# The softmax epsilon as a 65th column of the exponentials, in a kernel of attention, gated MoE and a second MoE

## The chip, the cores and the metric

One NeuronCore of a Trainium2 chip runs the whole program. The metric is the device time of one launch in microseconds (us). The engines that the text names are TensorE (PE, matrix products and transposes), VectorE (DVE), ScalarE (ACT), GpSimd (POOL) and SyncE (SP, which here only issues DMAs). All data are fp32; the large products run as three products of split numbers (a high and a low part).

## The reference

The first stage is the one that the change touches. Each batch entry and head has 768 queries, cut into chunks of 32; a chunk attends to a context of 56 keys (16 to the left, its own 32, 8 to the right) and to 8 memory keys, so 64 columns per head and query.

```python
scores = scale * np.matmul(q_c, k_full.transpose(0, 1, 3, 2))
scores = scores - np.max(scores, axis=-1, keepdims=True)
a = np.exp(scores)
a = a / (np.sum(a, axis=-1, keepdims=True) + 1e-09)
out[:, :, c_start:c_end] = np.matmul(a, v_full)
...
gate = 1.0 / (1.0 + np.exp(-(x @ w_gate)))
val = x @ w_val
x = gate * val @ w_out
...
h = x @ w_in
g = h * (1.0 / (1.0 + np.exp(-1.702 * h)))
return (g @ w_out).astype(np.float32)
```

There are 4 batch entries and 8 heads of width 64. The two later stages work on 3072 rows of width 512, with inner widths of 1536 and 2048.

## The kernel before

**Attention.** The function `attention` works on one of 32 tiles: 96 query rows, all 8 heads. PE transposes q and k (L436, L444), ACT copies them out of PSUM into `qt` and `kt` (L451, L456, L457), and PE computes the scores into the pair of PSUM banks `both` (L555). Then DVE takes the row maximum (L572) and subtracts it into the SBUF tile `e`, [96, 2, 4, 64] floats (L575); ACT makes exponentials of `e` in place (L580); DVE sums them per row and head into `sm` (L612), adds 1e-9 (L614) and inverts `sm` (L615). POOL, and for one 32-row band DVE, multiply `e` by `sm` into the padded tile `pw` (L623); PE transposes that (L645), ACT copies it to `pt` (L652), and PE multiplies by v (L704). The result is split into a high part on ACT (`xh`, L758) and a low part on DVE (`xl`, L761).

**Stages.** The six tiles of the first row block are the prologue. They have buffers of their own (`pro_bufs`, L886 to L892, where `pw` is cleared), except that the first of them uses the `e` of the set `main` (L870). The first product of the gated MoE (`first_product`, L821 and L828) needs all of them. From there on PE runs dense: gate and value products, the gate on ACT and DVE (L845, L848, L853), the output product (`gemm2`, L1020), and later the second MoE, whose two products are done in Strassen's manner (L1318, L1655). The other 26 tiles run beside this dense work, and all use the one `e` of `main`. Results of the gated MoE go out through two stages `f2`, used in turn: ACT copies a PSUM bank into a stage (L1040) and issues its store to `y_dram` (L1044).

**What sets the order.** All instructions are handed to a planner, the class `Schedule`. Each gets an engine, an estimated duration and keys that it reads and writes; the planner works out due times from the end backwards, simulates the engines by those estimates, and writes out one fixed order per engine. So each engine's queue is static, and one changed estimate can move instructions everywhere. Into gaps that the planner expects on PE ahead of the first product it puts fill products (L885), whose results nobody reads; their number is fixed in the program. In the trace one fill shows as two records.

SBUF is handed out in the order in which tiles are asked for. `e` of `main` is followed by `mx`, `sm`, `pt`, a pad of 112 floats (L871), and then by the slots of the weights and of what takes their place later. So all of these stand behind `e` at fixed distances.

Of the kernel before, what the change touches and what calls it, by code (L numbers as in the profile page):

```python
# [14 lines left out]
AF = mybir.ActivationFunctionType  # L15
ALU = mybir.AluOpType
# [6 lines left out]
TQ = CH * NCK  # L23
# [10 lines left out]
class Schedule:  # L34
# [9 lines left out]
    def add(self, eng, dur, fn, r=(), w=(), nbytes=0, due=None, slack=0.0, margin=0.0, hold=0.0):  # L44
        i = len(self.tasks)
        deps = set()
        for x in r:
            if x in self.writer:
                deps.add(self.writer[x])
        for x in w:  # L50
            if x in self.writer:
                deps.add(self.writer[x])
            deps.update(self.readers.get(x, ()))
        for x in r:
            self.readers.setdefault(x, set()).add(i)
        for x in w:
            self.writer[x] = i
            self.readers[x] = set()
        deps.discard(i)
        self.tasks.append(  # L60
            dict(eng=eng, dur=dur, fn=fn, deps=deps, nbytes=nbytes, due=due, slack=slack, margin=margin, hold=hold, succ=[])
        )
        return i
# [82 lines left out]
def kernel(  # L146
# [14 lines left out]
    nc = tc.nc  # L161
# [8 lines left out]
    NP = H // 2  # L170
    TPB = S // TQ
    NTILE = B * TPB
    KW = CTX + NM
    assert TK + NM == P and KW == 2 * CH and D == 2 * CH
    SCALE = 1.0 / float(D) ** 0.5
# [176 lines left out]
    class Bufs:  # L352


        def __init__(self, pool, suf, names, base=None):
            shapes = {
                "qn": [TQ, H, D],
                "kn": [P, H, D],
                "vn": [P, H, D],
                "qt": [P, NP, TQ],  # L360
                "kt": [P, NP, NCK, KW],
                "e": [TQ, 2, NP, KW],
                "mx": [TQ, 2, NP, 1],
                "sm": [TQ, H, 1],
                "pw": [TQ, H, P],
                "pt": [P, H, TQ],
                "qb": [P, NP, NCK, CH],
                "kb": [P, NP, 2 * NCK + 1, CH],
                "mn": [P, NP, CH],
                "mt": [P, NP, CH],  # L370
                "pn": [TQ, H, 3 * CH],
            }
            self.t = dict(base.t) if base else {}
            self.k = dict(base.k) if base else {}
            for n in names:
                self.t[n] = pool.tile(shapes[n], F32, tag=n + suf, name=n + suf)
                self.k[n] = n + suf
# [12 lines left out]
    def attention(t, bufs, banks, pe_path, extra=None, nth=0, last=False):  # L390
# [8 lines left out]
        kk = bufs.k  # L399
        T = bufs.t  # L400

        def tadd(eng, dur, fn, r=(), w=(), more=0.0, **kw):
            add(eng, dur, fn, r=r, w=w, slack=SL + more, **kw)
# [63 lines left out]
        else:  # L467
# [35 lines left out]
            if fresh:  # L503
                for hp in range(2):
# [9 lines left out]
                    w=[kk["mt"]],  # L514
# [48 lines left out]
        def scores():  # L563
            return both[:TQ, :, : NP * KW].rearrange("s a (p k) -> s a p k", k=KW)
# [8 lines left out]

        def ev_sub():
            nc.vector.tensor_tensor(  # L575
                out=T["e"], in0=scores(), in1=T["mx"].to_broadcast([TQ, 2, NP, KW]), op=ALU.subtract
            )

        def ev_exp():
            nc.scalar.activation(T["e"], T["e"], AF.Exp, scale=SCALE)  # L580

        def e3():
            return T["e"].rearrange("s a p k -> s (a p) k")
# [5 lines left out]
        else:  # L589
# [16 lines left out]
        d_sm = 0.64 if pe_path else 0.68  # L606
        tadd("dve", d_sm + edge, ev_max, r=kb01, w=[(kk["mx"], 0)])
        tadd("dve", d_sm, ev_sub, r=kb01 + [(kk["mx"], 0)], w=[(kk["e"], 0), (kk["e"], 1)])
        ke = [(kk["e"], 0), (kk["e"], 1)]
        tadd("act", c_act(512), ev_exp, w=ke)  # L610
        tadd(
            "dve", 0.6, lambda: nc.vector.tensor_reduce(out=T["sm"], in_=e3(), axis=AX.X, op=ALU.add), r=ke, w=[kk["sm"]]  # L612
        )
        tadd("dve", 0.07, lambda: nc.vector.tensor_scalar_add(T["sm"], T["sm"], 1e-9), w=[kk["sm"]])  # L614
        tadd("dve", 0.12, lambda: nc.vector.reciprocal(T["sm"], T["sm"]), w=[kk["sm"]])  # L615

        L = TQ - CH
# [269 lines left out]
    for i in range(NPRO):  # L887
        names = ["qn", "kn", "pw"] + (["vn", "qt", "kt", "e", "mx", "sm", "pt"] if i else [])
        x = Bufs(pro, f"_{i}", names, None if i else main)
        x.gate, x.ident, x.kid = None, lambda: ident["pro"], "ident"  # L890
        pro_bufs.append(x)
        (nc.gpsimd if i < 2 else nc.vector).memset(x.t["pw"], 0.0)  # L892

    pa = Bufs(pro, "", [], main)
    pa.k.update(qn="qn_a", kn="kn_a", pw="pw_a")
# [2 lines left out]
    for i in range(4):  # L898
        x = Bufs(pro, "", [], main)
# [52 lines left out]
    def attend(ts, bufs, banks):  # L952
        for t in ts:
            attention(t, bufs(t), banks(t), True)
# [25 lines left out]
    for i in range(2):  # L980
        for blk in (0, 2 * NCK):
            x = pb[2 * i]
# [18 lines left out]
    def attention_b(b):  # L1001
        for t in waves[b]:
            n = walk.index(t)
            before = walk[n - 1] if n else None
            x = pb[(t // 2) % 2 * 2 + t % 2]
            head = before is None or t % 2 == 0
            fresh = before is None or before // TPB != t // TPB
            extra = (0 if head else NCK, 2 - t % 2 if head else 0, fresh)
            attention(t, x, (A0, A1), False, extra, n, n == len(walk) - 1)
# [536 lines left out]
    a0, e, bb, a1 = sets[0]  # L1546
# [285 lines left out]
    a0, e, bb, a1 = AB  # L1832
# [67 lines left out]
```

## Time and profile before

| what | us |
|---|---|
| three runs | 1128.82, 1130.36, 1129.59 |
| median | 1129.59 |
| the profiled execution, its own time | 1130.38 |
| its span, from the first to the last instruction | 1128.6 |
| PE busy (99% of the span) | 1116.4 |
| DVE busy (75%) | 842.4 |
| ACT busy (52%) | 589.6 |
| POOL busy (14%) | 161.6 |
| first product of the dense phase starts at | 36.55 |

The mean granted clock of PE is 0.999 of full speed (2.4 GHz). Start times below count from the start of the span. An instruction's length can overlap the next one's start by about 0.1 us, since engines are pipelined: what an instruction takes of its engine's time is best read from its start to the next start.

### The profile page before, as it was taken

What the parts mean: (1) busy time and instruction counts of PE and PEld (TensorE: products, weight loads), DVE (VectorE), ACT (ScalarE), POOL (GpSimd) and SP (SyncE); (2) the same over time, 40 slices, a digit from 0 to 9 for tenths busy, and PEclk for the clock granted to TensorE, in tenths of its full rate; (3) what the DMA queues carried; (4) which work ended last, traced back from release to release, by engine and by line L of the source; (5) the groups of instructions that cost most, each with busy time, mean ns of one, the idle gap of its engine ahead of it and who ended that gap; (6) DMA issues with size and microseconds to landing.
All of it is one profiled execution on the core that took longest, in us unless ns stands there. A gap on an engine that the chain in (4) does not pass through costs nothing.

```text
span 1128.6 us, 19515 instructions
## 1 busy us (share of the span) xinstructions
PE 1116.4 (99%) x7190; PEld 933.7 (83%) x7190; DVE 842.4 (75%) x1440; ACT 589.6 (52%) x972; POOL 161.6 (14%) x209
## 2 busy tenths in 40 slices
PE   7999999999999999999999999999999999999998
PEld 6888899997888888888888888888888888888886
DVE  7989746776767788888887788869966369575365
ACT  5888632222222344676666777666455365354452
POOL 4332244122333113200001110000000000000000
PEclk9999999999999999999999999999999999999999
DMA  9676344335433555542556867868796666776526
GB/s 208 203 216 196 90 122 114 52 67 119 102 83 79 150 145 174 199 161 104 177 178 245 305 216 269 271 244 295 245 255 211 200 203 219 233 216 204 170 86 176
DMA packets 245903, 203.13 MB, mean 180 GB/s; under 512 B 170928, under 2 KB 191920, under 8 KB 245808
## 3 DMA queue, kind: packets, MB, share of 16 engines
q1 hardware_dynamic: 201560, 162.29, 48.9%
q0 software_dynamic: 6880, 24.12, 5.7%
q10 hardware_dynamic: 37368, 15.47, 5.0%
q8 instruction: 57, 0.93, 0.3%
q14 instruction: 38, 0.31, 0.1%
HBM read 151.49 MB, written 50.33 MB: 179 GB/s over the span
## 4 chain that ended last, share of the span: by engine, by line
PE 97%; DMA 1%; SPq 1%; ACT 0%; DVE 0%; issue 0%; ACTq 0%
PE bank L1318 30%; PE bank L1655 20%; PE bank L1020 18%; PE bank L821 15%; PE bank L828 8%; PE both L704 2%; PE both L555 2%; SPq L350 1%; PE bank L704 1%; PE bank L885 0%; DMA kn<-in_mem_k_dram 0%; PE bank L645 0%; DMA vn<-in_v_dram 0%; DMA w<-wo_dram 0%; PE both L645 0%
## 5 line engine op out<-in xcount | busy, mean ns | idle before, releaser
L1318 PE MATMUL bank<-sb_x,sb_r 128*128 128x512 f32 x1512 | 347.4, 389 | 0.0
L1318 PEld LDWEIGHTS bank<-sb_x,sb_r 128*128 128x128 f32 x1512 | 283.8, 188 | 58.9
L1655 PE MATMUL bank<-wq,w 128*128 128x512 f32 x756 | 178.0, 389 | 0.4 <-DMA w<-wo_dram 0.4
L1655 PEld LDWEIGHTS bank<-wq,w 128*128 128x128 f32 x756 | 141.8, 188 | 30.3 <-issue 0.8
L821 PE MATMUL bank<-xh,w 128*128 128x512 f32 (+1 forms) x464 | 159.6, 355 | 0.0
L821 PE MATMUL bank<-xl,w 128*128 128x512 f32 (+1 forms) x464 | 158.6, 353 | 0.0
L1334 DVE TENSOR_TENSOR sb_s<-bank,sb_s 128x512 f32<-128x512 f32 x108 | 74.4, 690 | 83.0 <-PE bank L1318 75.8
L828 PE MATMUL bank<-xh,w 128*128 128x512 f32 (+1 forms) x464 | 108.8, 356 | 0.0
L1020 PE MATMUL bank<-gh,wq 128*128 128x512 f32 (+1 forms) x448 | 98.7, 360 | 0.0
L821 PEld LDWEIGHTS bank<-xh,w 128*128 128x128 f32 x464 | 87.8, 189 | 12.6
L821 PEld LDWEIGHTS bank<-xl,w 128*128 128x128 f32 x464 | 87.8, 189 | 11.9
L1330 ACT ACTIVATE sb_s<-bank 128x512 f32<-128x512 f32 x108 | 64.8, 604 | 50.7 <-PE bank L1318 49.9
L828 PEld LDWEIGHTS bank<-xh,w 128*128 128x128 f32 x464 | 78.1, 189 | 12.4
L1020 PEld LDWEIGHTS bank<-gh,wq 128*128 128x128 f32 x448 | 76.4, 189 | 12.9
L670 DVE STREAM_TRANSPOSE pt<-raw 32x256 f32<-32x256 f32 x184 | 79.5, 432 | 4.7 <-POOL raw L623 2.1
L1626 DVE TENSOR_TENSOR wq<-xh_g,wq 128x1024 fp32r<-128x1024 f32 (+1 forms) x60 | 60.5, 1008 | 22.9 <-ACT wq L1623 22.5
L1623 ACT ACTIVATE wq<-xh_g 128x1024 fp32r<-128x1024 f32 (+1 forms) x60 | 53.3, 889 | 35.2 <-PE bank L1655 34.2
L853 ACT ACTIVATE gh<-sig 128x512 fp32r<-128x512 f32 (+1 forms) x58 | 32.3, 557 | 67.4 <-DVE sig L848 61.6
L623 POOL TENSOR_TENSOR raw<-e,sm 96x448 f32<-96x448 f32 (+2 forms) x69 | 41.0, 606 | 176.1 <-DVE sm L615 149.0
L1655 PE MATMUL bank<-wq,w_e 128*128 128x512 f32 x252 | 62.5, 389 | 0.0
L845 ACT ACTIVATE sig<-bank 128x512 f32<-128x512 f32 (+1 forms) x58 | 30.5, 526 | 55.5 <-PE bank L828 49.7
L1655 PEld LDWEIGHTS bank<-wq,w_e 128*128 128x128 f32 x252 | 47.3, 188 | 9.8
(215 smaller groups left out, 1646.1 us busy)
## 6 DMA issues: line engine op xcount, KB each, us to landing
sb_r<-wc_dram SPq DMA_DIRECT2D x133, 256.0 KB
w<-wo_dram SPq DMA_DIRECT2D x63, 512.0 KB
w_e<-wo_dram SPq DMA_DIRECT2D x21, 512.0 KB
wc_dram<-sb_r SPq DMA_DIRECT2D x15, 512.0 KB
wo_dram<-w POOLq DMA_DIRECT2D x14, 512.0 KB, 3.9
raw<-in_moe_w_out_dram SPq DMA_DIRECT2D x13, 512.0 KB
raw<-in_moe_w_in_dram SPq DMA_DIRECT2D x13, 512.0 KB
wf_dram<-f POOLq DMA_DIRECT2D x24, 256.0 KB, 2.9
```

The costliest lines, as they stand in the source:

```text
L623: eng.tensor_tensor(out=dst, in0=e3()[r, :, c], in1=T["sm"][r].to_broadcast([n, H, keys[1] - keys[0]]), op=ALU.mult)
L670: nc.vector.transpose(T["pt"][r * CH : (r + 1) * CH, :, c * CH : (c + 1) * CH], T["pn"][c * CH : (c + 1) * CH, :, kb * CH : (kb + 1) * CH],)
L704: nc.tensor.matmul((bk if to is None else to)[hp * D : (hp + 1) * D, o : o + q], T["vn"][:, 2 * p + hp, :], T["pt"][:, hp * NP + p, :q], s ...
L821: nc.tensor.matmul(bank[bk][:, :n], w[:, 0, ts[t]], x[xb][:, t, c0 : c0 + n], start=t == 0 and x is xhs, stop=False)
L828: nc.tensor.matmul(bank[bk][:, :n], w[:, 1, ts[t]], xhs[xb][:, t, c0 : c0 + n], start=False, stop=t == NK - 1)
L1020: nc.tensor.matmul(bank[into[m]][:, c0 : c0 + n], w[:, wi, m * P : (m + 1) * P], g[:, :n], start=f == 0 and j == 0 and c0 == 0, stop=f == ...
L1318: nc.tensor.matmul(bank[bk], w[:, o : o + P], xt[x, k][:, xl, :], start=first and k == 0 and wl == 0 and xl == 0, stop=k == 1 and wl == 1, ...
L1330: add("act", c_act(BLK), lambda: nc.scalar.activation(work[n], bank[bk], AF.Copy), r=[("bank", bk)], w=[n])
L1334: nc.vector.tensor_tensor(out=work[n], in0=bank[bk], in1=work[n], op=ALU.add)
L1623: nc.scalar.activation(quad[b_][:, c, 0, :], src(js), AF.Copy)
L1626: nc.vector.tensor_tensor(out=quad[b_][:, c, 1, :], in0=src(js), in1=quad[b_][:, c, 0, :].bitcast(F32), op=ALU.subtract)
L1655: nc.tensor.matmul(bank[bk], lhs, quad[b_][:, x, gl_, :], start=begin, stop=last and x == js[-1] and wl == 1, skip_group_check=not first,)
```

## The change

The tile `e` becomes 65 columns wide per head. The subtraction and the exponential write columns 0 to 63 through the view `e4()`. Column 64 holds the constant 1e-9, set once per buffer by a small memset on DVE ahead of everything else (six buffers: the five of the prologue and `main`'s, which the 26 later tiles share). The sum reads 65 columns, and the addition (L614) and its estimate in the planner are gone.

```diff
-                "e": [TQ, 2, NP, KW],
+                "e": [TQ, 2, NP, KW + 1],
...
         def ev_sub():
             nc.vector.tensor_tensor(
-                out=T["e"], in0=scores(), in1=T["mx"].to_broadcast([TQ, 2, NP, KW]), op=ALU.subtract
+                out=e4(), in0=scores(), in1=T["mx"].to_broadcast([TQ, 2, NP, KW]), op=ALU.subtract
             )
 
         def ev_exp():
-            nc.scalar.activation(T["e"], T["e"], AF.Exp, scale=SCALE)
+            nc.scalar.activation(e4(), e4(), AF.Exp, scale=SCALE)
+
+        def e4():
+            return T["e"][:, :, :, 0:KW]
...
-        tadd("dve", 0.07, lambda: nc.vector.tensor_scalar_add(T["sm"], T["sm"], 1e-9), w=[kk["sm"]])
         tadd("dve", 0.12, lambda: nc.vector.reciprocal(T["sm"], T["sm"]), w=[kk["sm"]])
...
         (nc.gpsimd if i < 2 else nc.vector).memset(x.t["pw"], 0.0)
+        nc.vector.memset(x.t["e"][:, :, :, KW : KW + 1], 1e-9)
```

Two things follow from it that the diff does not show. `e` takes 2080 bytes of each partition rather than 2048, so every tile behind `main`'s `e` stands 32 bytes further on. And the planner writes another order. Line numbers behind the change are 2 or 3 higher (the sum is L612 before and L615 after, the inversion L615 and L617, the fills L885 and L887).

DVE, the first three tiles of the prologue, before (`e`, `e_129`, `e_140` are the exponentials of tiles 0, 1 and 2, and so with `mx` and `sm`):

```order
9 L572 TENSOR_REDUCE mx_130<-both 96x8
10 L614 TENSOR_SCALAR sm<-sm 96x8
11 L575 TENSOR_TENSOR e_129<-both,mx_130 96x512
12 L615 RECIPROCAL sm<-sm 96x8
13 L612 TENSOR_REDUCE sm_131<-e_129 96x8
14 L572 TENSOR_REDUCE mx_141<-both 96x8
15 L614 TENSOR_SCALAR sm_131<-sm_131 96x8
16 L575 TENSOR_TENSOR e_140<-both,mx_141 96x512
17 L615 RECIPROCAL sm_131<-sm_131 96x8
```

The same place after (`e_130` and `e_142` are now those of tiles 1 and 2):

```order
15 L572 TENSOR_REDUCE mx_131<-both 96x8
16 L617 RECIPROCAL sm<-sm 96x8
17 L575 TENSOR_TENSOR e_130<-both,mx_131 96x8x64
18 L615 TENSOR_REDUCE sm_132<-e_130 96x8
19 L572 TENSOR_REDUCE mx_143<-both 96x8
20 L617 RECIPROCAL sm_132<-sm_132 96x8
21 L575 TENSOR_TENSOR e_142<-both,mx_143 96x8x64
```

The inversion now stands where the addition stood, ahead of the next tile's subtraction rather than behind it. The six memsets are rows 1 to 10 of DVE's queue, between those of `pw`.

PE, tiles 3 and 4 of the prologue, before (`pw_121` and `pw_125` are the probabilities of tiles 0 and 1, `qn_156`/`kn_157` q and k of tile 4, the L555 of row 23 its scores):

```order
17 L555 MATMUL both<-kt_150,qt_149 32x64 x24
18 L436 MATMUL bank_70<-ident,qn_156 128x96 x4
19 L444 MATMUL bank_71<-ident,kn_157 128x128 x4
20 L645 MATMUL bank_72<-ident,pw_121 128x96 x4
21 L645 MATMUL bank_73<-ident,pw_121 128x96 x4
22 L885 MATMUL bank_69<-ident 128x128
23 L555 MATMUL both<-kt_161,qt_160 32x64 x24
24 L704 MATMUL bank_68<-pt,vn 64x96 x8
25 L645 MATMUL bank_72<-ident,pw_125 128x96 x4
26 L645 MATMUL bank_73<-ident,pw_125 128x96 x4
```

After:

```order
17 L555 MATMUL both<-kt_153,qt_152 32x64 x24
18 L647 MATMUL bank_72<-ident,pw_121 128x96 x4
19 L647 MATMUL bank_73<-ident,pw_121 128x96 x4
20 L444 MATMUL bank_71<-ident,kn_161 128x128 x4
21 L436 MATMUL bank_70<-ident,qn_160 128x96 x4
22 L706 MATMUL bank_68<-pt,vn 64x96 x8
23 L647 MATMUL bank_72<-ident,pw_126 128x96 x4
24 L647 MATMUL bank_73<-ident,pw_126 128x96 x4
25 L555 MATMUL both<-kt_165,qt_164 32x64 x24
```

The transposes of tile 0's probabilities move ahead of those of tile 4's q and k, its scores behind tile 1's probabilities, and a fill goes. Over the whole prologue PE's queue has 33 fills after and 35 before; all other products are the same in number.

ACT at about 675 us of the trace before, where one row block of the gated MoE leaves through the two stages `f2` (here `f_83`) beside the first products of the second MoE (L1330 copies their banks out, L1841 works on their results):

```order
698 L296 ACTIVATE f_81<-raw_79 128x512
699 L1841 ACTIVATE xh_g<-sb_s_5380 128x512
700 L1841 ACTIVATE xl_g<-sb_s_5381 128x512
701 L1330 ACTIVATE sb_s_5380<-bank_73 128x512
702 L1330 ACTIVATE sb_s_5382<-bank_71 128x512
703 L1044 DMA y_dram<-f_83 128x512
704 L1040 ACTIVATE f_83<-bank_5332 128x512
705 L1261 ACTIVATE sb_r_5372<-f_81 128x2x256
706 L1841 ACTIVATE xh_g<-sb_s_5380 128x512
707 L1330 ACTIVATE sb_s_5381<-bank_73 128x512
```

After (L1043 and L1047 are the copy into a stage and its store):

```order
697 L296 ACTIVATE f_81<-raw_79 128x512
698 L1047 DMA y_dram<-f_83 128x512
699 L1043 ACTIVATE f_83<-bank_5305 128x512
700 L1844 ACTIVATE xh_g<-sb_s_5338 128x512
701 L1844 ACTIVATE xl_g<-sb_s_5339 128x512
702 L1333 ACTIVATE sb_s_5338<-bank_73 128x512
703 L1333 ACTIVATE sb_s_5340<-bank_71 128x512
704 L1264 ACTIVATE sb_r_5344<-f_81 128x2x256
705 L1844 ACTIVATE xh_g<-sb_s_5338 128x512
706 L1043 ACTIVATE f_83<-bank_5304 128x512
707 L1333 ACTIVATE sb_s_5338<-bank_70 128x512
708 L1333 ACTIVATE sb_s_5339<-bank_73 128x512
```

The first store is issued four instructions earlier, and the third copy into a stage (row 706), which stood at row 714 before, now stands ahead of two copies that free banks for PE.

## Rows read from the trace of the kernel before

**Rows 1.** The page: busy time by engine, and the chain that ended last

```profile
PE 1116.4 (99%) x7190; PEld 933.7 (83%) x7190; DVE 842.4 (75%) x1440; ACT 589.6 (52%) x972; POOL 161.6 (14%) x209
...
PE 97%; DMA 1%; SPq 1%; ACT 0%; DVE 0%; issue 0%; ACTq 0%
```

**Rows 2.** Waits of PE, all of the span: us, times, longest us

```profile
PE both L555 <- DVE sm L615: 1.0, 1, 1.0
PE bank L1020 <- ACT f L1040: 0.9, 1, 0.9
...
PE bank L1655 <- DMA w<-wo_dram: 0.4, 1, 0.4
```

**Rows 3.** Stretches: length, then busy us of each engine, clock, DMA share, GB/s

```profile
20.00:30.00 10.00, 9.77 (x204) 8.41 (x187) 9.28 (x20) 6.95 (x16) 7.73 (x8) 1.00 0.99 292
...
36.60:280.00 243.40, 243.40 (x2161) 213.80 (x2161) 184.12 (x355) 118.93 (x215) 71.85 (x83) 1.00 0.50 131
...
700.00:1122.00 422.00, 421.62 (x1860) 348.75 (x1859) 288.57 (x371) 215.62 (x311) 0.57 (x2) 1.00 0.69 218
```

**Rows 4.** Line L614 alone in two stretches: length, DVE busy (count), clock, DMA share, GB/s

```profile
0.00:36.50 36.50, 1.71 (x6) 1.00 0.83 194
36.50:1128.60 1092.10, 4.20 (x26) 1.00 0.59 180
```

**Rows 5.** Timeline of DVE, 0 to 34 us: start, length, line, tiles

```profile
7.96 0.17 DVE L569 MEMSET both<- 32x128 f32 x1 [2.81 <-PE both L555]
...
14.07 0.69 DVE L572 TENSOR_REDUCE mx<-both 96x8 f32<-96x512 f32 x1 [0.41 <-PE both L555]
14.68 0.83 DVE L614 TENSOR_SCALAR sm<-sm 96x8 f32<-96x8 f32 x1
15.42 0.68 DVE L575 TENSOR_TENSOR e<-both,mx 96x512 f32<-96x512 f32 x1
16.02 0.18 DVE L615 RECIPROCAL sm<-sm 96x8 f32<-96x8 f32 x1
...
23.02 0.20 DVE L615 RECIPROCAL sm<-sm 96x8 f32<-96x8 f32 x1
```

**Rows 6.** Timeline of POOL, same stretch and columns

```profile
12.58 3.27 POOL L623 TENSOR_TENSOR pw<-e,sm 32x448 f32<-32x448 f32 x4 [9.50 <-ACT qt L451]
...
20.05 5.60 POOL L623 TENSOR_TENSOR pw<-e,sm 32x448 f32<-32x448 f32 x6 [1.33 <-DVE sm L615]
```

**Rows 7.** Chain of waits, 0 to 45 us: start, length, what

```profile
14.76 0.75 DVE sm L614
...
16.25 0.86 PE both L555 x47
...
27.56 1.14 PE bank L885 x10
```

**Rows 8.** Timeline of ACT, 270 to 283 us

```profile
275.60 0.46 ACTq L350 DMA_DIRECT2D vn<-in_v_dram  x1
...
280.46 0.63 ACT L853 ACTIVATE gh<-sig 128x512 fp32r<-128x512 f32 x1 [2.72 <-DMA vn<-in_v_dram]
```

**Rows 9.** Timeline of ACT, 673 to 690 us

```profile
675.19 0.67 ACT L296 ACTIVATE f<-raw 128x512 f32<-128x512 f32 x1
...
677.24 0.36 ACTq L1044 DMA_DIRECT2D y_dram<-f  x1
...
680.01 0.60 ACT L1330 ACTIVATE sb_s<-bank 128x512 f32<-128x512 f32 x1
...
685.05 0.59 ACT L1040 ACTIVATE f<-bank 128x512 f32<-128x512 f32 x1
```

**Rows 10.** The page: DMA issues of this size, KB each, median us to landing

```profile
wf_dram<-f POOLq DMA_DIRECT2D x24, 256.0 KB, 2.9
```

**Rows 11.** DMA by queue, 149 to 153 us: packets, MB, share of 16 engines

```profile
q10 hardware_dynamic: 144, 0.26, 17.2%
```

**Rows 12.** DMA by queue, 1060 to 1090 us

```profile
q1 hardware_dynamic: 914, 1.80, 20.3%
```

## The prediction, made before the change was run

> **What bounds the kernel now.** I read the page first. PE is busy for 1116.4 of 1128.6 us, and 97% of the chain that ended last is PE's [rows 1]. DVE, where the change takes work away, is busy for three quarters of the span. So an operation on DVE matters only where PE waits for it. The waits of PE say where that is [rows 2]: one wait of 1.0 us for DVE's `sm` in the prologue, then 0.9 us for ACT's copy into a stage of `f2` and 0.4 us for a weight load. The stretches confirm it [rows 3]: from the first dense product to 280 us PE is busy for 243.40 of 243.40 us, and from 700 to 1122 us for all but 0.38. In 20 to 30 us, in the prologue, DVE is busy for 9.28 of 10 us and PE for 9.77. The addition L614 itself [rows 4]: six of its 32 instances, 1.71 us, lie in the prologue; the other 26, 4.20 us, lie beside a PE that does not wait for DVE. Their removal is worth nothing at the end, because PE's dense products cover it. What is left is the prologue: the first dense product starts when the six tiles are through, and what that start gains the end can gain, unless a later wait gives it back.
>
> **The additions in the prologue.** One of them is long: the second took 0.83 us [rows 5]. The chain of waits runs through it [rows 7]: 0.75 us of L614, then the subtraction L575, then PE's next scores at 16.25. In the changed order the inversion stands there instead. It took 0.18 and 0.20 us [rows 5], so 0.2 to 0.25 with its start, and the subtraction comes 0.75 - 0.25 = 0.5 us earlier.
>
> Would the inversion take over the long wait? During the 0.83 us POOL was at L623, from 12.58 on for 3.27 us [rows 6], but the inversion at 23.02 also ran while POOL was at L623 (20.05 to 25.65) and took 0.20. So I take 0.25 and keep 0.83 as the far end, at which this gain is zero.
>
> The Trainium skill (SBUF — State Buffer, Who interferes with whom) says that `tensor_scalar` can enter a mode in which it wants the port pair that DVE shares with GpSimd, an exclusive lock, while an operation with one SBUF input outside those modes does not contend. By that rule L614 was waiting for the lock, and the inversion would be free of it only if it has no such mode, which the page does not say of it. The trace agrees with the first half by the 0.83 us.
>
> The other five additions take 1.71 - 0.83 = 0.88 us together. DVE is 93% busy there, so they push all that follows on DVE; but from 20 us on PE is as full [rows 3], and the chain then runs through PE, fills among it [rows 7], so they shorten the end only where PE is brought forward as well. Between 0 and 0.88 I take 0.35, the nearer half, because PE's share is the higher one.
>
> **Fills.** Ten records of a fill take 1.14 us [rows 7], so one of two records takes 0.23. There are two fewer: 0.46 us of PE time in the part of the chain that is PE alone. It counts in full if what the fills waited beside comes earlier too, else not at all. DVE's work does come earlier, so I take 0.46.
>
> **What is added.** Six memsets on DVE, each no longer than the 0.17 us of the small memset at 7.96 [rows 5], so 1.0 us at most. That row shows 2.81 us of idle time ahead of it, in which DVE waits for the first scores: they are covered. Without that cover they would cost the 1.0 us. The sum over 65 columns rather than 64 reads 520 instead of 512 numbers; a reduction over 512 took 0.69, so 0.01 each, 0.06 for six. The subtraction now writes eight pieces of 64 rather than one run, and the exponential reads and writes such pieces. The maximum L572 already reads in such pieces, from PSUM, and its 0.69 us for 512 numbers is about the 0.68 of the subtraction L575 [rows 5], whose SBUF side is one run. So I take nothing for the pieces; the far end is 0.02 for each of three operations, 0.36 over six tiles.
>
> Sum of the prologue: -0.5 - 0.35 - 0.46 + 0.06 = about -1.25 us; the ends are 0.36 + 0.06 = +0.4 (nothing won, all small costs paid) and -0.5 - 0.88 - 0.46 = -1.85.
>
> **What is given back.** Two later waits end with a DMA. At 280.46 ACT had waited 2.72 us for a load of `vn` that was issued at 275.60 [rows 8], and its late copy then held PE for the 0.9 us of [rows 2]. At 793 us PE waits 0.4 us for weights. If a load is issued by a queue that moves with PE, the wait stays as it is; if its time is set by other transfers, the wait grows by up to the 1.25 us that PE is early. The load at 275.60 is issued behind copies that follow PE's products, so most of it moves; the weights at 793 wait for slots that PE frees. I take a quarter of the gain at each, 0.3 us; the ends are 0 and 1.25 for the first wait alone (which would eat it all).
>
> Sum: -1.25 + 0.6 = about -0.65 us, against the profiled execution's own 1130.38, so 1129.7 for that. The profiled execution stands 0.8 us above the median of the runs; the median moves from 1129.59 to about **1129.0 us**. A measurement of this kernel can tell about 0.2%, 2.26 us, from no change, and I forecast no such difference.
>
> **The rivals.**
>
> *A new wait at the stages of `f2`.* In the changed order the third copy into a stage stands ahead of two copies that free banks for the products L1318, and it needs the first store to have left its stage. The first store comes right behind L296, which ran at 675.19 [rows 9], so I estimate its issue at 675. Behind it, seven ACT instructions of about half a microsecond lie ahead of the third copy, some 4 us. The copy of the bank that comes next ran at 680.01 before, so PE needs it soon after 680. The point from which this decides is a landing time of about 5 us. How long a 256 KB store takes there has two bounds: 2.9 us, the median of the like stores of POOL [rows 10], and 7.8 us, from the store at 677.24 to the copy at 685.05 that uses the same stage. At 7.8 PE loses 2.8 us, and with the gain of 0.65 the kernel comes out at +2.15: 1131.7. For it: the SP queue loads weights there at the same time. Against it: the store now goes out before those loads and not behind them, so I estimate 4 us, between the bounds and nearer to the lower one. Chance 0.17, of which a third passes the 2.26 us together with some other small wait.
>
> *The 32 bytes.* All weight slots and rings behind `e` no longer start where they did, at multiples of 2048 bytes. The Trainium skill (DMA: Bandwidth & Descriptors, How a descriptor splits into AXI transactions) says that a descriptor that does not start at a multiple of 256 bytes is cut into one transaction more, which fetches bytes that go unused; by it a row of 2048 bytes becomes nine transactions instead of eight. As a mechanism here: transfers take up to an eighth longer, and PE begins to wait for weights. DMA is at 0.69 from 700 to 1122 us [rows 3], so on average an eighth more, 0.78, still fits; it would cost where the engines are full, about a tenth of the span, and there a few per cent: +1 to +5 us, so 1130 to 1134. Against it speaks a pair of rows. The stages `f2` already start 128 bytes off a multiple of 256 (the tiles ahead of them add up so), and a store from them, alone on its queue, took 0.172 x 16 x 4 = 11.0 engine-microseconds for 0.26 MB [rows 11], 24 KB per us. The loads of 1060 to 1090 us into aligned rings took 0.203 x 16 x 30 = 97 for 1.80 MB [rows 12], 18 KB per us. The one that is off is not slower, though one goes out and the other comes in. Chance 0.08.
>
> *More than the sum.* The prologue may be bound by DVE to its end. Then all 1.71 us, the two fills and the earlier POOL work that follows an earlier inversion add up, -2.2 at most, and nothing is given back: 1127.3. For it: DVE's 9.28 of 10 us. Against it: the two later waits, of which one ends with a DMA that was there before. Chance 0.12, a third of that beyond 2.26 us with luck in the order.
>
> *Nothing in the prologue either.* If the loads set the prologue's pace, or the inversion takes the long wait over, the start of the dense phase stays where it is and only small costs remain: 1129.6 to 1130. The DMA engines are at 0.99 of their time from 20 to 30 us [rows 3], which speaks for it; that the chain of waits runs through DVE and PE at 14.76 to 27.56 [rows 7] speaks against it. Chance 0.13. That the change doesn't do what it says (the constant overwritten, so that it must be set again) I exclude: nothing but the memset writes column 64.
>
> **How the numbers follow.** My case, -0.65 with ends of -1.85 and +0.4, has a chance of 0.50; by itself it spans 1127.7 to 1130.0. The range must reach to the rivals until 0.2 is left out: below to 1127.3, above to the `f2` wait in full, 1131.5. Left out are most of the transfers' case, a little of the `f2` case and whatever the new order does at a place that I don't see. Slower by over 0.2% (above 1131.85): 0.06 from the stages, 0.05 from the 32 bytes, 0.03 for an unseen place: 0.14. Faster by over 0.2% (below 1127.33): 0.04 of the larger gain and 0.04 for an unseen place: 0.08. Within: 0.78.
>
> **What would show it.** Right: the first dense product (L823 by its new number) starts at about 35.3 us instead of 36.55; on DVE no instruction between maximum and subtraction takes 0.8 us near 14.7; the six memsets end before 7; PE's waits after 37 us are those of [rows 2], the two later ones 0.2 to 0.4 us longer, and there is nothing at 680. Wrong: an inversion of 0.8 us; the first product at 36.5; a wait of PE for a copy of a bank at about 680 us, with ACT waiting for `y_dram`; waits of PE for weights at many places, or packets that take longer than before; a sum of more than 0.7 us.

## The result, and the profile after

The changed kernel takes **1142.9 us** (median, 1142.33 to 1143.59), the kernel before 1129.2 in the same comparison: the ratio is 1.0123, with a 95% interval of 1.0111 to 1.0135. The change is 13.7 us slower; the forecast was 1129.0, with a range to 1131.5.

The page of the profile after (its execution took 1142.84 us, span 1141.0), busy time by engine and the chain that ended last; they answer to [rows 1]:

```profile
PE 1128.2 (99%) x7186; PEld 935.0 (82%) x7186; DVE 839.0 (74%) x1414; ACT 589.6 (52%) x972; POOL 158.5 (14%) x209
...
PE 92%; SPq 3%; DMA 2%; DVE 2%; issue 0%; ACT 0%; ACTq 0%; DVEq 0%
```

PE is busy for 12 us longer and still for 99% of the span. It has the same products to do, two fills fewer. So most of the time did not go into waits; the products themselves take longer. The waits of PE after (us in total, times, longest us), beside [rows 2]:

```profile
PE bank L444 <- DMA kn<-in_mem_k_dram: 1.8, 1, 1.8
...
PE bank L436 <- DMA qn<-in_q_dram: 1.3, 1, 1.3
PE bank L647 <- DVE pw L625: 1.1, 1, 1.1
PE bank L1023 <- ACT f L1043: 0.8, 1, 0.8
```

The wait for DVE's `sm` is gone from the list, as forecast. Instead PE waits longer for the keys and queries of the prologue, 1.8 and 1.3 us. The stretches (length, busy us of PE, PEld, DVE, ACT, POOL, granted clock, DMA share, GB/s), beside [rows 3]:

```profile
8.00:20.00 12.00, 9.53 (x232) 8.01 (x231) 7.50 (x14) 5.86 (x14) 5.26 (x6) 0.87 1.18 160
20.00:30.00 10.00, 9.86 (x201) 8.65 (x200) 8.54 (x17) 8.19 (x19) 5.31 (x7) 0.99 1.13 201
...
36.60:280.00 243.40, 243.15 (x2173) 211.29 (x2172) 181.26 (x344) 121.33 (x218) 70.06 (x81) 1.00 0.50 126
700.00:1122.00 422.00, 421.86 (x1861) 348.70 (x1860) 292.10 (x375) 223.87 (x327) 0.57 (x2) 1.00 0.68 218
```

The first of these stretches before:

```profile
8.00:20.00 12.00, 8.58 (x224) 7.39 (x227) 9.98 (x20) 7.93 (x18) 5.36 (x6) 1.00 1.04 193
```

Two things stand out: in 8 to 20 us the granted clock is 0.87 instead of 1.00, and 20 to 30 us moves 201 GB/s at a DMA share of 1.13, where before 292 GB/s went through at 0.99. Set side by side product by product, the dense products start 2.9 us late (39.47 instead of 36.55 us), fall behind by 9 us more up to about 700 us, and from there on stay 12 us behind. So there are two losses: one in the prologue, one in the gated MoE.

**The gated MoE.** These are groups of PE's products by line and form, of the kernel before (line, tiles, partitions x columns, count, busy us, mean ns of one, idle us):

```profile
L1318 PE MATMUL bank<-sb_x,sb_r 128*128 128x512 f32 x1512 | 347.4, 389 | 0.0
...
L821 PE MATMUL bank<-xh,w 128*128 128x512 f32 x304 | 119.3, 392 | 0.0
...
L828 PE MATMUL bank<-xh,w 128*128 128x512 f32 x304 | 82.8, 394 | 0.0
L1020 PE MATMUL bank<-gh,wq 128*128 128x512 f32 x320 | 80.2, 391 | 0.0
...
L821 PE MATMUL bank<-xh,w 128*128 128x256 f32 x160 | 40.3, 284 | 0.0
```

And after:

```profile
L1321 PE MATMUL bank<-sb_x,sb_r 128*128 128x512 f32 x1512 | 347.5, 389 | 0.0
...
L823 PE MATMUL bank<-xh,w 128*128 128x512 f32 x304 | 121.0, 398 | 0.0
...
L830 PE MATMUL bank<-xh,w 128*128 128x512 f32 x304 | 84.6, 400 | 0.0
L1023 PE MATMUL bank<-gh,wq 128*128 128x512 f32 x320 | 82.6, 398 | 0.0
...
L823 PE MATMUL bank<-xh,w 128*128 128x256 f32 x160 | 39.9, 282 | 0.0
```

The products of 512 columns with `xh` or `gh` on one side and `w` or `wq` on the other take about 6 ns longer each; from start to start they now come every 233 ns or so (232 to 235 by group) instead of 227. In the same trace the products L1321 of the second MoE, on `sb_x` and `sb_r`, keep their 389 ns. The products of 256 columns became 2 ns shorter. The granted clock from 36.6 us on is 1.00 in both kernels, so it is not the clock. What distinguishes the first group is where the tiles stand: `xh` and `gh` lie ahead of `main`'s `e` and did not move, `w` and `wq` lie behind it and moved by 32 bytes. `sb_x` and `sb_r` both lie behind and moved together. So far this is an argument; the runs below test it.

**The prologue.** The SP queue's loads from 0 to 8 us (queue: packets, MB, share of 16 engines), before:

```profile
q1 hardware_dynamic: 5333, 1.34, 82.0%
```

After:

```profile
q1 hardware_dynamic: 4143, 1.04, 93.8%
```

These are loads of q and k in pieces of 256 bytes. One piece took 0.820 x 16 x 8 / 5333 = 19.7 ns before and 0.938 x 16 x 8 / 4143 = 29.0 ns after. The targets of tiles 0 and 1 moved by 32 bytes, the later ones by more. The chain that ended last runs through these loads in both kernels (start, length), before:

```profile
7.87 4.73 DMA kn<-in_mem_k_dram
```

After:

```profile
9.87 5.40 DMA kn<-in_mem_k_dram
```

So the keys of tile 3 land at 12.60 us before and at 15.27 after. That is 2.7 us, nearly all of the 2.9 by which the dense products start late. On PE it shows as a wait (timeline of PE after: start, length, line, tiles):

```profile
15.41 0.63 PE L444 MATMUL bank<-ident,kn 128*128 128x128 f32 x4 [1.83 <-DMA kn<-in_mem_k_dram]
...
17.17 1.54 PE L887 MATMUL bank<-ident 128*128 128x128 f32 x6
18.64 1.09 PE L555 MATMUL both<-kt,qt 64*32 64x64 f32 x48
...
39.47 0.47 PE L823 MATMUL bank<-xh,w 128*128 128x512 f32 x1
```

PE stood idle for 1.83 us until the keys of tile 3, the fourth, landed. Then follow stretches with a lower granted clock (length, busy us of the engines, granted clock, DMA share, GB/s):

```profile
16.00:18.00 2.00, 2.00 (x57) 1.91 (x57) 1.26 (x3) 1.36 (x3) 1.25 (x3) 0.71 1.01 158
18.00:20.00 2.00, 2.00 (x54) 1.60 (x53) 2.00 (x4) 0.63 (x1) 1.87 (x2) 0.50 1.19 183
```

From 18 to 20 us PE ran at 0.50, its lower level of 1.2 GHz. The scores L555 at 18.64 took 1.09 us there and 0.74 at 15.97. The kernel before kept the full clock from 8 us on; its waits there are of 1.0 us at most. That the long wait brought the lower clock is not shown: one of the traces below has 0.50 from 8 to 11 us behind shorter waits. Nor does it explain the slowdown: the 2.7 us are lost ahead of it, and of the four executions of the changed kernel the one with a mean granted clock of 0.999 took 1142.33 us, the three at 0.997 and 0.998 took 1142.84 to 1143.59.

**The removal itself** did what the diff says (timeline of DVE after):

```profile
0.81 0.10 DVE L895 MEMSET e<- 96x8 f32 x2 [0.81 <-PEq L1887]
...
5.21 0.07 DVE L895 MEMSET e<- 96x8 f32 x1
9.59 0.17 DVE L569 MEMSET both<- 32x128 f32 x1 [4.31 <-PE both L555]
...
16.74 0.69 DVE L572 TENSOR_REDUCE mx<-both 96x8 f32<-96x512 f32 x1 [1.19 <-PE both L555]
17.35 0.19 DVE L617 RECIPROCAL sm<-sm 96x8 f32<-96x8 f32 x1
17.46 0.69 DVE L575 TENSOR_TENSOR e<-both,mx 96x512 f32<-96x512 f32 x1
```

The six memsets take 0.05 to 0.07 us each and end at 5.28, with an idle stretch of 4.31 us ahead of the first use. The inversion stands where the addition stood and takes 0.19 us.

### The profile page after: what moved, and what is told of

Same layout as the page of the kernel before. It is cut to its first block, busy times and chain, and to the rows that moved or that the text cites. A ratio compares the mean times of both kernels' runs of the same rounds, so it can differ in the third digit from the quotient of the medians.

```text
span 1141.0 us, 19486 instructions
## 1 busy us (share of the span) xinstructions
PE 1128.2 (99%) x7186; PEld 935.0 (82%) x7186; DVE 839.0 (74%) x1414; ACT 589.6 (52%) x972; POOL 158.5 (14%) x209
## 4 chain that ended last, share of the span: by engine, by line
PE 92%; SPq 3%; DMA 2%; DVE 2%; issue 0%; ACT 0%; ACTq 0%; DVEq 0%
PE bank L1321 30%; PE bank L1658 20%; PE bank L1023 17%; PE bank L823 14%; PE bank L830 7%; SPq L350 3%; PE both L706 2%; PE both L555 1%; DVE pt L672 1%; DMA raw<-in_k_dram 1%; DMA y_dram<-f 0%; DMA kn<-in_mem_k_dram 0%; PE bank L887 0%; PE bank L647 0%; DMA w<-wo_dram 0%
## 5 line engine op out<-in xcount | busy, mean ns | idle before, releaser
L1321 PE MATMUL bank<-sb_x,sb_r 128*128 128x512 f32 x1512 | 347.5, 389 | 0.0
L1321 PEld LDWEIGHTS bank<-sb_x,sb_r 128*128 128x128 f32 x1512 | 283.8, 188 | 59.5
L823 PE MATMUL bank<-xh,w 128*128 128x512 f32 (+1 forms) x464 | 160.9, 358 | 0.0
L830 PE MATMUL bank<-xh,w 128*128 128x512 f32 (+1 forms) x464 | 110.4, 360 | 0.0
L1629 DVE TENSOR_TENSOR wq<-xh_g,wq 128x1024 fp32r<-128x1024 f32 (+1 forms) x60 | 60.5, 1008 | 24.3 <-ACT wq L1626 24.2
L625 POOL TENSOR_TENSOR raw<-e,sm 96x448 f32<-96x448 f32 (+2 forms) x69 | 38.6, 569 | 183.9 <-DVE sm L617 153.6
```

The lines of the kernel that those rows point to most:

```text
L625: eng.tensor_tensor(out=dst, in0=e3()[r, :, c], in1=T["sm"][r].to_broadcast([n, H, keys[1] - keys[0]]), op=ALU.mult)
L823: nc.tensor.matmul(bank[bk][:, :n], w[:, 0, ts[t]], x[xb][:, t, c0 : c0 + n], start=t == 0 and x is xhs, stop=False)
L830: nc.tensor.matmul(bank[bk][:, :n], w[:, 1, ts[t]], xhs[xb][:, t, c0 : c0 + n], start=False, stop=t == NK - 1)
L1321: nc.tensor.matmul(bank[bk], w[:, o : o + P], xt[x, k][:, xl, :], start=first and k == 0 and wl == 0 and xl == 0, stop=k == 1 and wl == 1, ...
L1629: nc.vector.tensor_tensor(out=quad[b_][:, c, 1, :], in0=src(js), in1=quad[b_][:, c, 0, :].bitcast(F32), op=ALU.subtract)
```

## The experiments

Two theories were put against each other: that the 32 bytes cost the time (in the products and in the loads), or that the planner's new order does. All experiments on the kernel before leave its instructions and their order untouched; they only move tiles.

**Weights 32 bytes on, in the order of before.** The prologue's own buffers are moved 64 bytes.

```diff
-    cp.tile([P, 112], F32, tag="pad1", name="pad1")
+    cp.tile([P, 120], F32, tag="pad1", name="pad1")
...
     make_identity(nc, ident["pro"])
+    pro.tile([P, 8], F32, tag="pad2", name="pad2")
```

> The kernel before, its instructions and their order untouched; only the weight slots and the tiles behind them stand 32 bytes further on, and the prologue's own buffers 64 bytes. Address theory (products whose weights stand 32 bytes off a multiple of 64 are slower): the products of the gated MoE take about 233 ns from start to start instead of 227, the prologue is as before, and the time is about 9 us longer, 1138. Order theory (the new order of the planner costs the time): as before, 1129 to 1130.

Measured: 1140.49, ratio 1.0091 (1.0074 to 1.0108). The same group of products:

```profile
L821 PE MATMUL bank<-xh,w 128*128 128x512 f32 x304 | 121.0, 398 | 0.0
```

398 ns, as after. The order of the planner has no part in this loss. The prologue was 1.1 us late, which the expectation did not have: a load target 64 bytes off turned out no better than one 32 bytes off (25.9 ns for a piece here, 26.9 in the next run).

**Only the prologue's buffers 32 bytes on.**

```diff
     make_identity(nc, ident["pro"])
+    pro.tile([P, 8], F32, tag="pad2", name="pad2")
```

> The kernel before, in its order; only the prologue's own buffers stand 32 bytes further on. Address theory: the loads of the prologue, in pieces of 256 bytes, take about a third to a half longer each, the first dense product starts at 39.5 to 41 us instead of 36.55, the dense products keep 227 ns, and the time is 3 to 5 us longer, 1132 to 1134. Order theory: as before, 1129 to 1130.

Measured: 1132.51, ratio 1.0027 (1.0014 to 1.0041), so 3 us; single runs lie between 1130.68 and 1135.95. The products keep 392 ns. The loads of 0 to 8 us:

```profile
q1 hardware_dynamic: 4500, 1.13, 94.4%
```

That is 26.9 ns for a piece. The time came out as the address theory had it, the start of the dense products did not: 37.96 us in the trace, not 39.5 to 41. That trace is of one of the quicker executions (1130.86). The order theory again expected nothing here.

**Activations 32 bytes on, weights where they were; and both together.**

```diff
-    cp.tile([P, 224], F32, tag="pad0", name="pad0")
+    cp.tile([P, 232], F32, tag="pad0", name="pad0")
...
-    cp.tile([P, 112], F32, tag="pad1", name="pad1")
+    cp.tile([P, 104], F32, tag="pad1", name="pad1")
```

The second of the two leaves `pad1` at 112 and adds the pad of 8 floats to the prologue.

> The kernel before, in its order; now the activations (the moving operands of the gated MoE's products, and the main attention buffers) stand 32 bytes further on and the weights where they were. Relative theory (what counts is that the two operands of a product differ in where they start within 64 bytes): the gated MoE's products take about 233 ns instead of 227 and the time is about 9 us longer, 1139. Weight theory (only the weights' own start counts): 227 ns and 1129 to 1131.

> The kernel before, in its order; activations and weights both 32 bytes further on, so that the two stand to each other as before; the prologue's own buffers 64 bytes further on. Relative theory: 227 ns, and the time is that of before plus 1 us or so for the prologue, 1130 to 1132. Weight theory, and a theory by which either operand's own start counts: 233 ns and 1139 to 1141.

Measured: 1139.64, ratio 1.0099 (1.0083 to 1.0114), for the activations alone; 1132.7, ratio 1.0035 (1.0023 to 1.0048), for both. The products, activations alone:

```profile
L821 PE MATMUL bank<-xh,w 128*128 128x512 f32 x304 | 120.9, 398 | 0.0
```

Both moved:

```profile
L821 PE MATMUL bank<-xh,w 128*128 128x512 f32 x304 | 119.3, 392 | 0.0
```

So with these 32 bytes neither operand's own place matters, only how the two stand to each other; why that costs time, no run shows. The remaining 0.35% of the second run is more than the 1 us that was expected for its prologue. It agrees with the 0.27% of the prologue alone, since the intervals overlap; in its trace the first dense product starts 1.2 us late and the end is 1.3 us late. This is the trace with a granted clock of 0.50 from 8 to 11 us.

**How far apart they may stand.** Five runs make `pad1` larger, by 64 to 1024 bytes:

```diff
-    cp.tile([P, 112], F32, tag="pad1", name="pad1")
+    cp.tile([P, 128], F32, tag="pad1", name="pad1")
```

(128 floats are 64 bytes more; the other runs have 144, 176, 240 and 368.)

> The kernel before, in its order; weights and prologue buffers 64 bytes further on, activations as before. If a multiple of 64 bytes is enough for the products: 227 ns, 1130 to 1132, with the prologue 1 us late as in the run with the weights 32 bytes off. If the products need more (256 bytes, or the same place within 2048): above 230 ns, 1135 or more.

> As the run with 256 bytes, with 128 (the prologue's load targets stand 128 bytes further on as well). If the step is 128: 227 ns for the products, and 1129 to 1132. If it is 256: 233 ns, as with 32 and 64, and 1136 to 1140.

> The kernel before, in its order; the weights stand 256 bytes further on than before, the activations where they were; the prologue's load targets keep their places within 256 bytes. If 256 bytes is the step at which the two operands of a product have to stand alike: 227 ns from start to start and the time of before, 1129. If they have to stand alike within more (512, 1024 or 2048 bytes): above 230 ns and 1136 to 1140.

> As the run with 256 bytes, with 512. If the step is 512 or less: 227 ns, 1129. If it is more: above 230 ns, 1136 to 1140.

> As the run with 256 bytes, with 1024. If the step is 1024 or less: 227 ns, 1129. If it is 2048 (a row of 512 numbers, where all large tiles of the kernel before start): above 230 ns, 1136 to 1140.

| weights moved by, bytes | time, us | ratio to before | 95% interval |
|---|---|---|---|
| 64 | 1137.64 | 1.0084 | 1.0068 to 1.01 |
| 128 | 1139.72 | 1.0088 | 1.0071 to 1.0105 |
| 256 | 1128.98 | 0.9998 | 0.9985 to 1.001 |
| 512 | 1129.63 | 1.0001 | 0.9991 to 1.0012 |
| 1024 | 1129.41 | 1.0007 | 0.9995 to 1.002 |

The same group with 128 bytes:

```profile
L821 PE MATMUL bank<-xh,w 128*128 128x512 f32 x304 | 121.0, 398 | 0.0
```

And with 256:

```profile
L821 PE MATMUL bank<-xh,w 128*128 128x512 f32 x304 | 119.3, 392 | 0.0
```

Of the distances tried, multiples of 256 bytes cost nothing, and 32, 64 and 128 bytes cost about the same.

**The changed kernel with its addresses put back.** First the weights alone, then the prologue's load targets as well, at multiples of 128 bytes, then these at multiples of 256:

```diff
-    cp.tile([P, 112], F32, tag="pad1", name="pad1")
+    cp.tile([P, 104], F32, tag="pad1", name="pad1")
...
                 self.t[n] = pool.tile(shapes[n], F32, tag=n + suf, name=n + suf)
+                if n == "e" and suf:
+                    pool.tile([P, 8], F32, tag="pade" + suf, name="pade" + suf)
```

The first has only the change of `pad1`; the third pads by 40 floats instead of 8.

> The changed kernel with a pad 32 bytes smaller behind the tile of exponentials, so that the weights stand where they stood before; of the prologue's buffers those of tiles 0, 1, 3 and 5 stand at multiples of 64 bytes again, those of tiles 2 and 4 do not. Address theory: dense products back at 227 ns, a prologue between that of before and that of the change, 1129 to 1132. Order theory: as the change, 1143.

> The changed kernel with the pad 32 bytes smaller and 32 bytes of padding behind each of the prologue's tiles of exponentials, so that weights and loads all start at multiples of 64 bytes. Address theory: what was forecast for the change by itself comes out, 1129.0, within 1 us of the kernel before and rather below it, with the first dense product at about 35.3 us. Order theory: as the change, 1143.

> The changed kernel in the planner's new order, weights where they were and all load targets of the prologue at multiples of 256 bytes. If the new order costs time at the late attention tiles (1.6 us at 440 to 460 us in the run with the addresses put back): first dense product 1.5 to 2 us earlier than in the kernel before, and the time within 1 us of before, rather above it. If the order costs nothing: 1.5 us shorter than before.

Measured: 1131.85, 1131.77 and 1131.65 us, with ratios of 1.0017 (1.0008 to 1.0026), 1.0014 (1.0005 to 1.0023) and 1.0017 (1.0005 to 1.0029). Of the 1.23% all but 0.14 to 0.17% is gone with a change of pads, some 12 us. The second was expected at 1129.0, and the third within 1 us of before: both miss. None is faster than before, although the first dense product starts at 35.05 to 35.4 us in all three, as forecast. Against the trace of before this gain is given back, and the largest part goes at the same place in the three traces. This is PE in the second one (timeline):

```profile
450.07 0.88 PE L708 MATMUL both<-pt,vn 128*64 128x96 f32 x16 [0.82 <-issue]
...
456.92 0.88 PE L708 MATMUL both<-pt,vn 128*64 128x96 f32 x16 [0.31 <-issue]
```

The first product of the probabilities and v for a late attention tile waited 0.82 us, the next 0.31. The profile names no releaser (`issue`); by the times it is work on DVE, here in the same kernel:

```profile
440.37 0.58 DVE L534 STREAM_TRANSPOSE qt<-f 128x384 f32<-128x384 f32 x1 [2.68 <-DMA x_dram<-qt]
...
443.97 0.42 DVE L1408 TENSOR_TENSOR p_t<-p_f 128x256 f32<-128x256 f32 x1
...
449.08 0.89 DVE L674 STREAM_TRANSPOSE pt<-raw 32x256 f32<-32x256 f32 x2
```

And in the kernel before:

```profile
439.95 0.58 DVE L532 STREAM_TRANSPOSE qt<-f 128x384 f32<-128x384 f32 x1 [1.43 <-DMA x_dram<-qt]
...
448.17 0.89 DVE L670 STREAM_TRANSPOSE pt<-raw 32x256 f32<-32x256 f32 x2
```

The last two transposes of the probabilities L674 (L670 before) end at 449.97 us, 0.1 us before PE goes on at 450.07; before, they ended at 449.06 and PE came to them at 449.75. They are late because the copy L1408 now stands ahead of the tile's maximum, and because the transpose of its q starts 0.42 us later, when its load has landed. So PE comes about half a microsecond earlier to a result that comes 0.9 us later. Over 440 to 460 us the three lose 1.5 to 1.7 us against the trace of before. The changed kernel itself shows no wait of PE there: its slower products leave DVE the time.

**The order of before, with the addition gone.** The planner keeps a task of 0.07 us that emits nothing. The first run has the load targets at multiples of 256 bytes (a pad of 40 floats), the second at those of before (56 floats).

```diff
-        tadd("dve", 0.07, lambda: nc.vector.tensor_scalar_add(T["sm"], T["sm"], 1e-9), w=[kk["sm"]])
+        tadd("dve", 0.07, lambda: None, w=[kk["sm"]])
```

> The changed kernel, addresses as in the run with 256 bytes, and with a task of 0.07 us and no instruction left in the planner where the addition was, so that all other instructions keep the order of before. Order theory for the rest: no waits at 440 to 460 us, the gain of the prologue stays, and the time is 1 to 2 us shorter than before. If the rest comes from the wider sum or the pieces of 64 columns: no gain, or a loss.

> The changed kernel in the order of before, weights and load targets at the same places within 256 bytes as before: the removal of the additions (and the wider sums, the pieces and the six memsets) alone. By the forecast's terms without the fills: 0.5 to 1.2 us earlier at the first dense product, 0.3 to 1 us shorter than before at the end. If removing them is worth nothing: as before.

Measured: 1128.0, ratio 0.9989 (0.9977 to 1.0002), and 1128.72, ratio 0.9994 (0.998 to 1.0007). The first differs from the last of the three runs above (1.0017) in the order alone, and their intervals don't touch: so the order is the cause of that loss. The place at 450 us is not all of it: the last products of these two traces end 4.0 us apart, of which 1.7 arise at 440 to 460 us and the rest in steps of up to 0.7 at other places, which stay unexplained. A wait at 450 us can come in the order of before too: five of the thirteen traces in that order show one of 0.2 to 1.3 us, and the second run here has that of 1.3. In the new order, with quick products, each of the three traces shows it. What the removal is worth by itself, the second run, can't be told from nothing.

**Load targets of the prologue at multiples of 256 bytes, nothing else.**

```diff
                 self.t[n] = pool.tile(shapes[n], F32, tag=n + suf, name=n + suf)
+                if n == "e" and suf:
+                    pool.tile([P, 48], F32, tag="pade" + suf, name="pade" + suf)
```

> The kernel before, in its order; padding brings every load target of the prologue to a multiple of 256 bytes (before, those of tiles 2, 3 and 4 stood 64, 128 and 192 bytes off one). If a load in pieces of 256 bytes is quick only from a multiple of 256 on: the loads of the tiles in the middle come sooner, PE's wait of 1.0 us for the keys of tile 2 goes, and the time is 0.3 to 1 us shorter than before. If a multiple of 64 is enough: as before.

Measured: 1128.04, ratio 0.9987 (0.9974 to 1.0). The loads of 0 to 8 us:

```profile
q1 hardware_dynamic: 5888, 1.47, 81.6%
```

And from 8 to 16 us, here and in the kernel before:

```profile
q1 hardware_dynamic: 7113, 1.78, 99.3%
```

```profile
q1 hardware_dynamic: 5549, 1.39, 104.8%
```

That is 17.7 and 17.9 ns for a piece, against 19.7 and 24.2 before, where the loads of the tiles in the middle are off. The loads did get faster, and PE's wait of 1.0 us for keys (of tile 3, not tile 2) is gone from its list. Whether the kernel does stays open: the interval ends at 1. No version here is shown to be faster than the kernel before.

## Why the prediction was wrong

- **The step that failed: the sum put the shift of 32 bytes at nothing.** It let PE's dense products and the prologue's loads take as long as before, and left the shift to a rival with a chance of 0.08, priced by transfers alone at 1 to 5 us. The runs showed two costs in its place, about 9 us in the products and about 3 in the prologue.
- **The loads.** The rival was weighed by transfers of 2048 bytes [rows 11, 12], and for those the finding holds: in the trace after, PE waits nowhere for weights. But the pieces that matter are the prologue's, of 256 bytes, and no row of them was read for it. The Trainium skill (DMA: Bandwidth & Descriptors, How a descriptor splits into AXI transactions) gives the split for any size. By it a piece of 256 bytes off a multiple of 256 becomes two transactions instead of one, which is a far larger share than nine for eight. That section of the Trainium skill gives no times and does not say whether this holds for the place that is written, which is what moved here. The runs agree with its direction: 17.7 ns for a piece from a multiple of 256, 26 to 29 ns otherwise. The slower pieces cost 3 us in the order of before. In the changed kernel the dense products start at 39.47 us, against 35.05 with the addresses put back and 36.55 in the trace of before.
- **A line that was passed over.** The prediction gave the waits of PE as one for DVE's `sm`, then the two later ones, and took the prologue for one that DVE and PE pace; that loads set its pace was a rival with a chance of 0.13. The same list has a wait as long as that for `sm`, for a load of the prologue:

```profile
PE bank L444 <- DMA kn<-in_mem_k_dram: 1.0, 1, 1.0
```

  With the chain through the loads up to 12.60 us, shown above, it says that slower loads delay PE at once.
- **That the products read both operands from places that moved against each other was not in the sum at all.** It costs about 9 us: 1656 records of 512 columns at 6.1 ns more are 10.1 us, less 720 records of 256 columns at 1.8 ns less, 1.3 us. The rows of the kernel before could not show it, since there all these tiles start at multiples of 2048 bytes. The two pads in the source, of 224 and 112 floats, were a hint that places count; the text ahead of the prediction names the second only as a neighbour.
- **The long addition, -0.5 us.** The mechanism (an addition that waits while POOL is at L623) may be right, but the size was that of one execution. In the run with the weights 512 bytes on, whose prologue is that of before, the same instruction took:

```profile
14.07 0.33 DVE L614 TENSOR_SCALAR sm<-sm 96x8 f32<-96x8 f32 x1
```

  Of the eleven traces with the addition in the order of before, seven show 0.29 to 0.34 us and four 0.53 to 0.83. The first dense product of the untouched prologue starts anywhere from 35.03 to 36.55 us in the four traces that have it. So a gain of 1.25 us against the one at 36.55 was no more than what differs from one execution to the next.
- **That the inversion would not take the long wait over** held. The run with the order of before and the addition gone, on DVE:

```profile
13.59 0.68 DVE L574 TENSOR_REDUCE mx<-both 96x8 f32<-96x512 f32 x1
14.30 0.69 DVE L577 TENSOR_TENSOR e<-both,mx 96x512 f32<-96x512 f32 x1
14.91 0.19 DVE L620 RECIPROCAL sm<-sm 96x8 f32<-96x8 f32 x1
```

- **The start of the dense phase**, forecast at 35.3 us, came out at 35.05 to 35.4 with the addresses put back.
- **What is given back**, forecast as 0.6 us at 280 and 793 us: 0.4 was lost at 280 in the second run with the addresses put back, nothing at 793. The 1.6 us at 440 to 460 us were not foreseen. An unseen place had a chance of a few in a hundred in the forecast, which looked at 280, 675 and 793 us only.
- **The new wait at the stages of `f2`** did not come: no trace of the new order shows PE waiting for a copy of a bank from 600 to 700 us.
- **The wider sum and the pieces** cost what was taken: 677 ns on average against the 667 ns that 512 columns take.

Together: in the two traces 2.9 us at the start and 9 in the products make 12, and the two profiled executions are 12.5 us apart (1142.84 and 1130.38). The medians are 13.7 apart because the profiled execution of before is 1.2 us slower than its median. Putting the addresses back gives 12.0 to 12.3 us by the ratios. How the two costs add is known to a microsecond or two only, since executions of one kernel differ by as much. The order's loss appears only once the products are quick again.

## What to carry to other kernels

A tile that grows by a few bytes moves every tile behind it, so look at the start addresses before and after, not only at the instructions. Keep the two operands of a product alike within 256 bytes, and the targets of loads in small pieces at multiples of 256; a few floats of padding gave some 12 of 13.7 us back here. And where a static planner writes the order, test a small edit in the old order first, by leaving an empty task in its place.

## What the runs showed that was not expected

- A product of 512 columns takes 6 ns longer (233 instead of 227 ns from start to start) where its two operands' starts differ by 32, 64 or 128 bytes within 256; differences of 256, 512 and 1024 bytes cost nothing. Moving both together by 32 bytes costs the products nothing. Products of 256 columns become shorter by the same shifts, by 1 to 3 ns for 32 or 128 bytes and about 5 for 64.
- In the first 8 us a 256-byte piece of a load takes 17.7 ns into a place at a multiple of 256 bytes and 26 to 27 ns at 32, 64 or 128 bytes off one (29 in the changed kernel). An offset of 32 bytes is hardly worse than one of 128.
- In the changed kernel 3.4 us at a granted clock of 0.50 began at 16.85 us, 1.4 us after a wait of PE of 1.83 us. Another trace has as long a stretch behind waits of at most 1.4 us, so the wait is not shown to be the cause.
